# A spectral network on one NeuronCore: the product of unit 0 moved from the small products' step to the head of the products to times, with an order edge

## The chip, the cores and the metric

The kernel runs on one core of one Trainium2 chip. The metric is the device time of one execution in microseconds (us); lower is better. Three runs of the kernel before took 821.88, 822.1 and 817.92 us, a median of 821.88 us. One more execution, the one that the profiler recorded, took 814.48 us; the time from its first to its last instruction (the span) is 812.7 us. All positions below are microseconds from the start of that span.

The engines are PE (TensorE, matrix products), DVE (VectorE), ACT (ScalarE), POOL (GpSimd) and SP, which issues the DMAs. Each works through a list of its own in order and waits at an instruction until what it needs is there.

## The reference, cut to what matters

```python
def A(x, w_r, w_i):                       # x is 2048 x 512
    X = rfft2(x) * (w_r + 1j * w_i)
    return irfft2(X, s=(2048, 512))

def B(u, log_A_real, A_imag, C_real, C_imag, log_dt, D_skip):
    dt = exp(log_dt)
    A = -exp(log_A_real) + 1j * A_imag
    C = (C_real + 1j * C_imag) * dt[:, None]
    P = exp((A * dt[:, None])[:, :, None] * arange(2048))
    K = 2.0 * einsum("dn,dnl->dl", C, P).real          # one long filter for each channel
    y = irfft(rfft(u.T, 4096) * rfft(K, 4096), 4096)[:, :2048]
    return y.T + u * D_skip

x = x + A(layernorm(x))
x = x + B(layernorm(x))
x = x + A(layernorm(x))
x = x + B(layernorm(x))
```

Layer A is a filter in the two-dimensional spectrum. Layer B convolves each of the 512 channels with its own filter, as a product of spectra. All inputs are float32.

## The kernel before

Every Fourier transform is written out as products with constant matrices. The work that the change touches is in layer B, `layer_b`, which runs twice. It goes over four blocks of 128 channels each. For one block:

1. **Rows forward** (four groups, from `forward_b`): PE multiplies the normalised rows with a constant (`p<-t,w` in the first layer B, `p<-t,x` in the second), and ACT copies the result to a tile `z` (L643).
2. **Turns**: eight transposes on DVE (L649).
3. **Pairs** (four: 0 to 3; the "small products' step" is what `weigh` does for one of them): PE multiplies the turned tile with the constant `mb` (`p<-z,mb`, two results for each pair); DVE multiplies them with the spectrum of the filter (L953, four products for each pair, in tiles `wb`; one more small one, L955, in pairs 0 and 2); and four half-tile sums and differences (L964, L965) make the product spectrum `Y`. One of these four is made on DVE and three on POOL, by a table of letters, `YB`. Pairs 0 and 1 fill the first half of `Y` (j = 0), pairs 2 and 3 the second half (j = 1).
4. **The product of unit 0** (L968): one small product with the constant `MIX`, which repairs column 0 of one half of `Y`, and a copy back by ACT (L969). It comes once for each half, and stands in `weigh` after pair 0 and after pair 2.
5. **Units**, the "products to times" (`units` in `back`): eight for each block, four for each half. A unit is 16 small products `p<-mb,u` and a copy by ACT (L978). A unit of a half needs both of its pairs and the repaired column 0.
6. **Rows back** (four groups, `p<-u,t`): PE, then DVE adds the result to the residual (L992).

What sets the order: `layer_b` hands lists of steps to `interleave`, which spreads the shorter ones evenly between the longer ones, three times for a block. First come pairs 0 and 1 with the rows of the next block and the rows back of the last one; then pairs 2 and 3 with the rest of the next block's rows and the first `UH` units; then the turns of the next block with the remaining units. A scheduler turns that into one list for each engine. `issue_after(x)` is an edge that makes an instruction stand behind `x` in its engine's list; it adds no waiting by itself. In the first layer B further steps are spread through these three places (`fill`): the rest of the making of the filters (`kernel_time`, with the lines L819 to L876) and the filters' own forward transforms (`kernel_freq`). The second layer B has no such filling.

The results of PE lie in PSUM buffers: in both layers B two for rows forward, three for pairs, and three that the product of unit 0, the units and the rows back share.

Of the kernel before, what the change touches and what calls it, by code (L numbers as in the profile page):

```python
# [55 lines left out]
WB = 7  # L56
FS = [0.22, 0.37]
FH = 0.7
UH = 6
YB = 'ggvgggvg'  # L60
RNP = 'g'
KP = 0
S1 = 0
# [185 lines left out]
class Net:  # L249
# [376 lines left out]
    def forward_b(self, src, T, tag="z"):  # L626

        nc = self.nc
        tiles = {}

        def rows(n0):


            if n0 == 0:
                tiles["z"] = self.sb("z", [64, 2, 2, 8, 2])
            xs = [src(n0 + i) for i in range(4)]
            ps = [self.ps("p1", [64, 2, 2, 2]) for b in range(2)]
            self.side_by_side([(ps[b][64 * c:64 * c + 64, :, j, m], xs[2 * m + c][64 * b:64 * b + 64, 64 * j:64 * j + 64],
                                T[64 * b:64 * b + 64, n0 + 2 * m + c].rearrange("p (u r) -> p u r", r=2))
                               for m in range(2) for j in range(2) for c in range(2) for b in range(2)])  # L640
            m = n0 // 2
            for b in range(2):
                nc.scalar.copy(tiles["z"][:, :, :, b, m:m + 2].rearrange("p u j m r -> p (u j) (m r)"),  # L643
                               ps[b].rearrange("p u j m r -> p (u j) (m r)"))

        def turn(u):
            if u == 0:
                tiles["zt"] = self.sb(tag, [64, 2, 32])
            nc.vector.transpose(tiles["zt"][:, u:u + 8].rearrange("p u j d -> p (u j d)"),  # L649
                                tiles["z"][:, u:u + 8].rearrange("p u j b m r -> p (u j b m r)"))  # L650

        MB = split(self.small[:, 0:256], "slm", [2, 2, 64])

        def pair(i, use):
            last = None
            for pl in range(2):
                p = self.ps("p2", [512])
                products = []
                for h in (1, 0):
                    o = p[64 * h:64 * h + 64].rearrange("p (u d) -> p u d", d=32)  # L660
                    u = 32 * (i % 2) + 16 * h
                    c = 1 if u == 0 else 0
                    z = tiles["zt"][:, :, i // 2]
                    products += [(o[:, 0], MB[:, 0, pl], z[:, 0])] * c + [(o[:, c:], MB[:, 1, pl], z[:, u + c:u + 16])]
                last = self.side_by_side(products, last)
                use(pl, p)

        return ([partial(rows, n0) for n0 in range(0, 16, 4)], [partial(turn, u) for u in range(0, 64, 8)],
                [partial(pair, i) for i in range(4)])
# [264 lines left out]
    def layer_b(self, kf, T, out, x=None, src=None, first=None, more=(), fill=(), switch=(), kept=None, after=None):  # L934
# [3 lines left out]
        nc = self.nc  # L938
# [5 lines left out]
        def weigh(blk, Y, pairs, i):  # L944
# [14 lines left out]
            for h in range(2):  # L959
# [3 lines left out]
                e = [nc.vector if c == "v" else eng for c in YB[i % 2 * 4 + 2 * h:i % 2 * 4 + 2 * h + 2]]  # L963
                e[0].tensor_sub(y[0:64], v[0, 0], v[1, 1])  # L964
                e[1].tensor_add(y[64:128], v[0, 1], v[1, 0])  # L965
            if i % 2 == 0:
                pm = self.ps("p3", [32])
                nc.tensor.matmul(pm, MIX, Y[:, :, i // 2, 0], start=True, stop=True)  # L968
                nc.scalar.copy(Y[:, :, i // 2, 0], pm)  # L969

        def back(blk, Y):
            V = self.sb("u", [32, 2, 2, 32])

            def units(j, d):
                p = self.ps("p3", [64, 8])
                self.side_by_side([(p[64 * r:64 * r + 64, :, i], Y[:, d + i, j], MBT[:, 64 * r:64 * r + 64])
                                   for i in range(8) for r in range(2)])
                nc.scalar.copy(V[:, :, j, :, d:d + 8].rearrange("p n q d -> p q n d"),  # L978
                               p.rearrange("p (q n) d -> p q n d", q=2))
# [29 lines left out]
        last = []  # L1009
# [188 lines left out]
```

## Time and profile before

| | us |
|---|---|
| median of three runs | 821.88 |
| profiled execution | 814.48 |
| its span | 812.7 |
| first layer A, with most of the filters' making | 0 to about 280 |
| first layer B with the rest of the filters | about 280 to 556 |
| second layer A | about 556 to 691 |
| second layer B, four blocks | 691 to 812.7 |

| engine | busy, us | share of the span |
|---|---|---|
| PE | 635.4 | 78% |
| DVE | 650.3 | 80% |
| ACT | 429.6 | 53% |
| POOL | 403.3 | 50% |

Busy time is summed over the whole span. The shares are means over stages with different limits, so which engine holds a stage back has to be read in that stage. In the rows of a timeline the columns are the start, how long the group took, the engine, the line, the operation, what is written and read with its shape, and how many instructions were merged; a bracket gives the idle time of the engine before it and what ended that.

### The profile page before, as it was taken

Reading aid. Unit: us, or ns where it says so; the run is one execution under the profiler, and the core shown is the slowest. Engines: PE = TensorE matmul, PEld = TensorE weight load, DVE = VectorE, ACT = ScalarE, POOL = GpSimd, SP = SyncE. Lnnn points to the kernel's source line nnn. Section 1 sums busy time; section 2 is a strip of 40 time slices with the busy share of each in tenths; the row PEclk is TensorE's granted clock in tenths of the full one; section 3 lists DMA queues with packets and bytes.
Section 4 is the critical chain, followed back from the end, with each engine's and each line's share of the span. In section 5 each row is a group of like instructions: output and inputs, shape, how many; then the busy total and the mean of one; then the engine's idle time right before and its main releaser. Section 6 shows DMA issues by size and latency. Waiting matters only on the chain. (4 is left out here: it accounts for less than half of the span.)

```text
span 812.7 us, 18848 instructions
## 1 busy us (share of the span) xinstructions
PE 635.4 (78%) x7232; PEld 442.6 (54%) x7232; DVE 650.3 (80%) x1307; ACT 429.6 (53%) x918; POOL 403.3 (50%) x594
## 2 busy tenths in 40 slices
PE   3347788896767877997789968665899896897786
PEld 2336666664444435653356637344877663475566
DVE  7999659799998969679797868667587796976783
ACT  3424778756566955776578614213765345233212
POOL 3675876746624154613366444180056571763752
PEclk9657999999989979999699989888999997999998
DMA  8200742353556331460335456303123013322512
GB/s 313 107 0 15 159 96 79 80 139 111 130 155 142 113 54 36 106 182 19 60 86 141 147 121 186 132 21 106 53 79 81 26 40 117 105 88 75 154 44 62
DMA packets 144609, 80.49 MB, mean 99 GB/s; under 512 B 78500, under 2 KB 124200, under 8 KB 143624
## 3 DMA queue, kind: packets, MB, share of 16 engines
q1 hardware_dynamic: 144264, 78.77, 35.0%
q8 instruction: 57, 0.93, 0.5%
q0 software_dynamic: 256, 0.52, 0.4%
q14 instruction: 32, 0.26, 0.1%
HBM read 54.77 MB, written 25.03 MB: 98 GB/s over the span
## 5 line engine op out<-in xcount | busy, mean ns | idle before, releaser
L965 POOL TENSOR_TENSOR u<-wb,wb 64x512 f32<-64x512 f32 x64 | 91.3, 1427 | 118.8 <-DVE wb L953 105.8
L318 PE MATMUL p<-z,mb 128*64 128x512 f32 (+1 forms) x480 | 106.2, 558 | 16.9 <-DVE z L649 9.7
L953 DVE TENSOR_TENSOR wb<-p,kk 128x512 f32<-128x512 f32 x128 | 81.2, 680 | 18.9 <-PE p L318 17.6
L864 PE MATMUL pv<-qp 128*64 128x128 f32 x1024 | 79.9, 295 | 13.8 <-DVE qp L853 10.8
L643 ACT COPY z<-p 128x512 f32<-128x512 f32 x96 | 51.7, 594 | 69.0 <-PE p L318 60.9
L853 DVE TENSOR_TENSOR qp<-qp,mag 128x1024 f32<-128x1024 f32 x64 | 84.4, 1324 | 0.9
L864 PEld LDWEIGHTS pv<-qp 128*64 128x64 f32 x1024 | 61.3, 145 | 40.3 <-issue 9.7
L318 PEld LDWEIGHTS p<-mb,u 128*64 128x64 f32 x2048 | 71.0, 150 | 20.3 <-POOL u L964 12.6
L318 PE MATMUL p<-mb,u 128*64 128x64 f32 x2048 | 74.1, 236 | 10.1 <-POOL u L964 9.6
L851 DVE SCALAR_TENSOR_TENSOR qp<-qp,mag 128x256 f32<-128x256 f32 x128 | 65.3, 527 | 16.2 <-ACT qp L794 15.9
L528 DVE TENSOR_TENSOR w<-wt,p 128x514 f32<-128x514 f32 x64 | 42.6, 687 | 32.0 <-PE p L318 25.2
L649 DVE STREAM_TRANSPOSE z<-z 128x512 f32<-128x512 f32 x96 | 58.3, 675 | 9.7 <-ACT z L643 9.6
L978 ACT COPY u<-p 128x512 f32<-128x512 f32 x64 | 37.6, 587 | 53.6 <-PE p L318 53.6
L533 POOL TENSOR_TENSOR w<-w,w 64x257 f32<-64x257 f32 x48 | 40.0, 834 | 51.4 <-DVE w L528 45.7
L318 PEld LDWEIGHTS p<-z,mb 128*64 128x64 f32 x480 | 36.0, 146 | 51.9 <-issue 26.9
L458 PE MATMUL p<-w,w 128*128 128x128 f32 x128 | 32.0, 428 | 41.1 <-DVE w L451 38.8
L1063 POOL TENSOR_SCALAR w<-w,norms 128x128 f32<-128x128 f32 x64 | 38.1, 606 | 38.3 <-DMA w<-h 38.1
L832 DVE TENSOR_SCALAR kw<-pk 128x512 bf16<-128x512 f32 x64 | 43.3, 681 | 11.8 <-PE pk L830 11.7
L458 PEld LDWEIGHTS p<-w,w 128*128 128x128 f32 x128 | 27.7, 318 | 45.2 <-issue 24.7
L794 ACT ACTIVATE kf<-pk 128x512 f32<-128x512 f32 x64 | 38.9, 607 | 22.0 <-PE pk L833 21.6
L964 POOL TENSOR_TENSOR u<-wb,wb 64x512 f32<-64x512 f32 x32 | 46.2, 1445 | 2.3
L794 ACT ACTIVATE qp<-kf,half 128x512 f32<-128x512 f32 x64 | 47.2, 738 | 0.0
(198 smaller groups left out, 1523.4 us busy)
## 6 DMA issues: line engine op xcount, KB each, us to landing
wt<-in_w SPq DMA_DIRECT2D x32, 257.0 KB
w<-h SPq DMA_DIRECT2D x32, 256.0 KB
kf<-kk SPq DMA_DIRECT2D x32, 256.0 KB
kk<-kf SPq DMA_DIRECT2D x32, 256.0 KB
u<-in_x SPq DMA_DIRECT2D x16, 256.0 KB
hr<-in_x SPq DMA_DIRECT2D x16, 256.0 KB
kt<-stage SPq DMA_DIRECT2D x32, 128.0 KB
h<-hr SPq DMA_DIRECT2D x16, 256.0 KB
```

What stands on the lines that cost most here:

```text
L318: last = self.nc.tensor.matmul(out, weights, data, start=True, stop=True, skip_group_check=True).ins
L458: nc.tensor.matmul(p[:, b], xf[:, b], t, start=True, stop=True)
L643: nc.scalar.copy(tiles["z"][:, :, :, b, m:m + 2].rearrange("p u j m r -> p (u j) (m r)"), ps[b].rearrange("p u j m r -> p (u j) (m r)"))
L649: nc.vector.transpose(tiles["zt"][:, u:u + 8].rearrange("p u j d -> p (u j d)"), tiles["z"][:, u:u + 8].rearrange("p u j b m r -> p (u j b ...
L794: last["x"] = nc.scalar.activation(*a, **k).ins
L832: nc.vector.tensor_scalar(whole, p, MAGIC, -MAGIC, op0=ALU.add, op1=ALU.add)
L851: nc.vector.scalar_tensor_tensor(QP[:, c, 0], QP[:, c, 1, :, ::-1], -1.0 if c else 1.0, m[:, 0], op0=ALU.mult, op1=ALU.mult)
L853: nc.vector.tensor_mul(t, t, mag[:, None, 1:3, 256 * j:256 * j + 256].to_broadcast([128, 2, 2, 256]))
L864: nc.tensor.matmul(p[64 * t:64 * t + 64, g], QP[:, c, 2, d:d + 2].rearrange("p s a -> p (s a)"), QP[:, c, 0:2, d:d + 2].rearrange("p k s b ...
L953: nc.vector.tensor_mul(split(m[c, pl], "du", [32, 16]), by_channel(p), split(k[c], "du", [32, 16]))
L964: e[0].tensor_sub(y[0:64], v[0, 0], v[1, 1])
L965: e[1].tensor_add(y[64:128], v[0, 1], v[1, 0])
```

## The change

The product of unit 0 and its copy leave `weigh`. They now stand at the head of the first unit of each half (d = 0), with an edge behind the last matrix product of the pair issued most recently (`self.paired`, set in `forward_b`). `UH` goes from 6 to 4: all four units of the second half now stand with the next block's turns. `YB` still gives one of the four sums of each pair to DVE, but it is now the difference of the tile's lower half (h = 0), where it was that of the upper half.

```diff
-UH = 6
-YB = 'ggvgggvg'
+UH = 4
+YB = 'vgggvggg'
...
                 last = self.side_by_side(products, last)
                 use(pl, p)
+            self.paired = last
...
                 e[0].tensor_sub(y[0:64], v[0, 0], v[1, 1])
                 e[1].tensor_add(y[64:128], v[0, 1], v[1, 0])
-            if i % 2 == 0:
-                pm = self.ps("p3", [32])
-                nc.tensor.matmul(pm, MIX, Y[:, :, i // 2, 0], start=True, stop=True)
-                nc.scalar.copy(Y[:, :, i // 2, 0], pm)
-
         def back(blk, Y):
             V = self.sb("u", [32, 2, 2, 32])

             def units(j, d):
+                if d == 0:
+
+                    pm = self.ps("p3", [32])
+                    with self.tc.issue_after(self.paired):
+                        nc.tensor.matmul(pm, MIX, Y[:, :, j, 0], start=True, stop=True)
+                    nc.scalar.copy(Y[:, :, j, 0], pm)
```

No instruction is added or taken away; their order on the engines changes. The lists are the same up to the middle of the first block of the first layer B.

First place: PE in the third block of the second layer B. `p<-mb,u` is a unit, `p<-u,mb` the product of unit 0 (here that of the second half), the two rows `p<-z,mb` are pair 3, and `p<-t,x` are rows forward of the next block, of which only the one next to the others is shown. Before:

```order
L318 MATMUL p_1758_8333<-t_6922,x_6926 64x64x2
L318 MATMUL p_1747_8286<-mb_2602,u_8149 64x64 x16
L968 MATMUL p_1756_8329<-u_8149,mb_2602 128x32
L318 MATMUL p_1759_8352<-mb_2602,u_8149 64x64 x16
L318 MATMUL p_1764_8410<-z_8104,mb_2602 64x512 x2
L318 MATMUL p_1767_8417<-z_8104,mb_2602 64x512 x2
L318 MATMUL p_1760_8370<-mb_2602,u_8149 64x64 x16
L318 MATMUL p_1761_8388<-mb_2602,u_8149 64x64 x16
L318 MATMUL p_1770_8428<-t_6922,x_6926 64x64x2
```

Behind the last row stand the rest of that group of rows forward and then the four units of the second half. In the changed kernel pair 3 stands behind three units of the first half, with no product of unit 0 ahead of it but that of the first half:

```order
L318 MATMUL p_1757_8330<-t_6922,x_6926 64x64x2
L318 MATMUL p_1747_8286<-mb_2602,u_8149 64x64 x16
L318 MATMUL p_1758_8349<-mb_2602,u_8149 64x64 x16
L318 MATMUL p_1759_8367<-mb_2602,u_8149 64x64 x16
L318 MATMUL p_1762_8389<-z_8065,mb_2602 64x512 x2
L318 MATMUL p_1765_8396<-z_8065,mb_2602 64x512 x2
L318 MATMUL p_1768_8407<-t_6922,x_6926 64x64x2
```

The group of rows forward that begins in the last row here is followed by the fourth unit of the first half, and only then comes the product of unit 0 of the second half (L975 in the changed file):

```order
L318 MATMUL p_1769_8408<-t_6922,x_6926 64x64x2
L318 MATMUL p_1770_8427<-mb_2602,u_8149 64x64 x16
L975 MATMUL p_1772_8447<-u_8149,mb_2602 128x32
L318 MATMUL p_1773_8450<-mb_2602,u_8149 64x64 x16
L318 MATMUL p_1774_8470<-mb_2602,u_8149 64x64 x16
L318 MATMUL p_1775_8490<-mb_2602,u_8149 64x64 x16
L318 MATMUL p_1776_8510<-mb_2602,u_8149 64x64 x16
L318 MATMUL p_1781_8545<-z_8445,mb_2602 64x512
```

So the product of unit 0 of the second half moved from ahead of pair 3 to behind it, and two more units of the first half stand ahead of pair 3. Ahead of these units the block has two groups of rows forward where it had three. In the second block one more group stands between L975 and the four units; that one is the third block's first, which the third block then no longer has.

Second place: PE at the end of the fourth block, where no rows forward follow. Pair 3, the units and the products of unit 0 stood like this:

```order
L318 MATMUL p_1815_8729<-z_8484,mb_2602 64x512 x2
L318 MATMUL p_1818_8736<-z_8484,mb_2602 64x512 x2
L318 MATMUL p_1800_8625<-mb_2602,u_8529 64x64 x16
L968 MATMUL p_1809_8668<-u_8529,mb_2602 128x32
L318 MATMUL p_1810_8671<-mb_2602,u_8529 64x64 x16
L318 MATMUL p_1811_8689<-mb_2602,u_8529 64x64 x16
L318 MATMUL p_1812_8707<-mb_2602,u_8529 64x64 x16
L318 MATMUL p_1821_8747<-mb_2602,u_8529 64x64 x16
```

Three more units of the second half follow. In the changed kernel all four units of the first half stand ahead of L975:

```order
L318 MATMUL p_1813_8708<-z_8445,mb_2602 64x512 x2
L318 MATMUL p_1816_8715<-z_8445,mb_2602 64x512 x2
L318 MATMUL p_1800_8625<-mb_2602,u_8529 64x64 x16
L318 MATMUL p_1809_8668<-mb_2602,u_8529 64x64 x16
L318 MATMUL p_1810_8686<-mb_2602,u_8529 64x64 x16
L318 MATMUL p_1819_8726<-mb_2602,u_8529 64x64 x16
L975 MATMUL p_1820_8744<-u_8529,mb_2602 128x32
L318 MATMUL p_1821_8747<-mb_2602,u_8529 64x64 x16
```

Three units moved ahead of the product of unit 0; the end of the fourth block of the first layer B changes in the same way.

Third place: PE early in the first block of the first layer B. `L833` (L834 in the changed file) is a product of the filters' making, on which ACT and then DVE go on. Before, the product of unit 0 of the first half stood ahead of it:

```order
L830 LDWEIGHTS th_2963
L830 MATMUL pk_3112<-kb_599,th_2963 128x256
L968 MATMUL p_729_3076<-u_3021,mb_2602 128x32
L833 LDWEIGHTS ni_601
L833 MATMUL pk_3050<-kw_3049,ni_601 128x512
L833 LDWEIGHTS ni_601
L833 MATMUL pk_3112<-kw_3111,ni_601 128x512
```

In the changed kernel it is gone from here:

```order
L831 LDWEIGHTS th_2963
L831 MATMUL pk_3109<-kb_599,th_2963 128x256
L834 LDWEIGHTS ni_601
L834 MATMUL pk_3050<-kw_3049,ni_601 128x512
L834 LDWEIGHTS ni_601
L834 MATMUL pk_3109<-kw_3108,ni_601 128x512
```

It moved some 70 rows further back, behind pair 1 and the group of products L865 (L864 before). On POOL the order in each pair stays two sums (L965) and one difference (L964). On DVE the difference of pair 0 now stands behind two of pair 1's products instead of ahead of them.

## The prediction

> **What bounds the kernel now.** I read the busy times of the page first, then the busy times by stage, then the waits of PE, then the timeline of one block, engine by engine. Over the whole span no engine is full:
>
> ```profile
> PE 635.4 (78%) x7232; PEld 442.6 (54%) x7232; DVE 650.3 (80%) x1307; ACT 429.6 (53%) x918; POOL 403.3 (50%) x594
> ```
>
> The stages differ. The columns are the stretch, its length, the busy us (and instructions) of PE, weight loads, DVE, ACT and POOL, PE's granted clock, the DMA share and GB/s:
>
> ```profile
> 400.00:440.00 40.00, 35.42 (x552) 23.89 (x552) 35.85 (x51) 29.32 (x56) 25.70 (x25) 0.91 0.41 94
> 722.00:752.00 30.00, 25.69 (x494) 18.30 (x492) 22.38 (x35) 9.41 (x18) 16.63 (x13) 0.94 0.36 108
> ```
>
> In the first layer B, with its filling, PE and DVE are both near 90%. In the second layer B (one block in the second row) PE is busy 25.69 of 30 us, DVE 22.38 and POOL 16.63: nobody is full, so a chain of waits sets the time. The waits of PE in the second layer B (who waited for whom, us in total, times, longest):
>
> ```profile
> PE p L968 <- POOL u L964: 10.7, 5, 3.2
> PE p L318 <- POOL u L964: 6.5, 4, 2.6
> ```
>
> PE waits 17.2 us for POOL, most of it at the product of unit 0. One block shows how. It begins at 747.26 with pair 0 and the next begins at 777.63:
>
> ```profile
> 747.26 2.01 PE L318 MATMUL p<-z,mb 128*64 128x32 f32 x12
> 749.20 1.10 PE L318 MATMUL p<-t,x 64*64 64x128 f32 x32
> ...
> 760.30 1.15 PE L318 MATMUL p<-mb,u 128*64 128x64 f32 x32
> 763.58 0.42 PE L968 MATMUL p<-u,mb 128*128 128x32 f32 x2 [2.12 <-POOL u L964]
> 763.93 1.15 PE L318 MATMUL p<-mb,u 128*64 128x64 f32 x32
> 764.91 1.89 PE L318 MATMUL p<-z,mb 128*64 128x512 f32 x8
> ...
> 772.30 5.50 PE L318 MATMUL p<-mb,u 128*64 128x64 f32 x128 [2.60 <-POOL u L964]
> 777.63 2.87 PE L318 MATMUL p<-z,mb 128*64 128x32 f32 x16
> ```
>
> A unit is 32 instructions here. PE has the first unit done at 761.45, then stands at the product of unit 0 of the second half, which needs pair 2 from POOL; pair 3 (764.91), which needs nothing of that, stands behind it. POOL and DVE in the same block:
>
> ```profile
> 750.44 2.97 POOL L965 TENSOR_TENSOR u<-wb,wb 64x512 f32<-64x512 f32 x2 [7.02 <-DVE wb L953]
> 757.55 1.62 POOL L964 TENSOR_TENSOR u<-wb,wb 64x512 f32<-64x512 f32 x1
> 767.96 2.95 POOL L965 TENSOR_TENSOR u<-wb,wb 64x512 f32<-64x512 f32 x2 [4.43 <-DVE wb L953]
> 770.98 1.26 POOL L964 TENSOR_TENSOR u<-wb,wb 64x512 f32<-64x512 f32 x1
> 765.99 2.48 DVE L953 TENSOR_TENSOR wb<-p,kk 128x512 f32<-128x512 f32 x4 [3.61 <-PE p L318]
> ```
>
> POOL has pair 1 done at 757.55 + 1.62 = 759.17, then makes pair 2 and stands idle 4.43 us until DVE has products of pair 3 for it. So the loop is: POOL's pair 2, product of unit 0, a unit, pair 3 on PE, on DVE, on POOL, then the units of the second half. The block before shows the same places:
>
> ```profile
> 717.26 2.01 PE L318 MATMUL p<-z,mb 128*64 128x32 f32 x12
> 734.90 3.40 PE L318 MATMUL p<-z,mb 128*64 128x512 f32 x8
> 743.47 3.95 PE L318 MATMUL p<-mb,u 128*64 128x64 f32 x128 [2.10 <-POOL u L964]
> ```
>
> **Second and third block.** The change adds and removes no instruction; each of its edits is worth what it moves.
>
> Before, pair 3 starts 764.91 - 747.26 = 17.65 us into its block (734.90 - 717.26 = 17.64 in the other). In the changed list PE reaches pair 3 after what it did from 747.26 to 761.45 (14.19 us), less one group of rows forward (1.10), plus two more units at 3.95 / 4 = 0.99 each: 14.19 - 1.10 + 1.98 = **15.07 us**, 2.58 us sooner. The three units need pair 1 from POOL, ready at 759.17 - 747.26 = 11.91; PE comes to the first of them at 14.19 - 1.15 - 1.10 = 11.94, so they fit with nothing to spare. What follows pair 3 keeps its length: from its start to the units of the second half 772.30 - 764.91 = 7.39 us, and from these to the next block 747.26 - 743.47 = 3.79. The block becomes 15.07 + 7.39 + 3.79 = 26.25 us instead of 28.83 by the same rows. That is 2.58 us for each of two blocks, 5.2.
>
> The cover of the moved work: one group of rows forward, one unit and the product of unit 0 now run while POOL makes pair 3. They take about 1.1 + 1.0 + 0.4 of 7.39 us, beside pair 3's own 1.89, and in the second block one group more, 1.1. PE then waits once, 7.39 - 1.9 - 1.1 - 1.0 - 0.4 = 3.0 us in the third block and 1.9 in the second, where it waited twice. What is late next is POOL's pair 3, which no PE order shortens. If the cover were gone, the units would start later by what is left uncovered, at most these 3.6 us. The turns (eight on DVE) need the last rows forward, which in the second block move to just ahead of the units; their ACT copies and 4.87 us on DVE lie beside the wait and the four units:
>
> ```profile
> 770.85 4.87 DVE L649 STREAM_TRANSPOSE z<-z 128x512 f32<-128x512 f32 x8 [1.07 <-ACT z L643]
> ```
>
> Moving the DVE difference from the upper to the lower half keeps one on DVE and three POOL operations for each pair, and the sums that start first on POOL are the same; I cost it at nothing, with DVE's free 7.6 us of the 30 as cover. If it is not free, it costs a DVE difference ahead of pair 3's products, about 1.1 us a block. The edge is an order alone: nothing, and ACT's copy of unit 0 moves with the product. SP's issues of filter spectra and outputs are shuffled; the spectra are fetched a block ahead, so nothing again.
>
> Clock. Both blocks are longer than 28.83 (30.00 and 30.37), and the granted clock (the third figure from the end) says why:
>
> ```profile
> 734.00:738.00 4.00, 4.00 (x40) 1.78 (x42) 1.29 (x2) 0.80 (x2) 0.00 (x0) 0.64 0.18 47
> 772.00:778.00 6.00, 5.70 (x132) 5.59 (x134) 3.72 (x7) 1.91 (x4) 0.24 (x1) 0.72 0.01 3
> 795.00:800.00 5.00, 5.00 (x98) 5.00 (x98) 1.07 (x1) 1.29 (x3) 3.42 (x3) 0.50 0.01 3
> ```
>
> Two of the four waits were followed by a slow stretch. The first stretched 734.90 to 743.47 to 8.57 instead of 7.39 (1.18 us), the second 772.30 to 777.63 to 5.33 instead of 3.79 (1.54 us). With one wait a block I keep the second, since the third block's wait gets longer, and take back the first: 1.2.
>
> **First block and the ends.** In the first block of the second layer POOL is never idle, so its units of the second half start when POOL is done, as before: nothing. At the end of the fourth block:
>
> ```profile
> 794.23 0.64 PE L968 MATMUL p<-u,mb 128*128 128x32 f32 x2 [3.24 <-POOL u L964]
> 794.80 9.09 PE L318 MATMUL p<-mb,u 128*64 128x64 f32 x224
> 797.29 1.26 POOL L964 TENSOR_TENSOR u<-wb,wb 64x512 f32<-64x512 f32 x1
> ```
>
> POOL ends at 798.55, the units at 803.89. The changed list does the first half's four units while POOL makes pair 2, and the second half's from 798.55. At full clock these take 3.95 and end at 802.5, 1.4 us sooner; at the clock of the row 795 to 800 (98 instructions in 5 us, 1.63 us a unit) they end at 805.1, 1.2 later. The wait ahead of them grows from 3.24 to about 4 us, and 3.24 was followed by a clock of 0.50, so I take nothing, and -1.4 to +1.2 as bounds, here and at the end of the first layer B, which has the same rows.
>
> The Trainium skill bears on this ("TensorE: Matmul & The Clock Gate", Part 1): after an idle window of about 3.4 us the array falls to half clock and needs about as long of sustained work to come back. By that rule the ends would cost about 1.2 us each rather than nothing. The trace agrees with the 3.24 us row, but it also shows 0.64 behind a wait of 2.12, which is shorter than the rule's window.
>
> **First layer B, with the filling.** The first product of unit 0 stands ahead of products of the filters' making, on which ACT and then DVE wait; a later one likewise:
>
> ```profile
> 293.40 0.41 PE L968 MATMUL p<-u,mb 128*128 128x32 f32 x2 [1.24 <-POOL u L964]
> 294.13 0.60 ACT L794 ACTIVATE kf<-pk 128x512 f32<-128x512 f32 x1
> 296.67 0.42 DVE L851 SCALAR_TENSOR_TENSOR qp<-qp,mag 128x256 f32<-128x256 f32 x1 [3.40 <-ACT qp L794]
> 416.42 0.67 DVE L832 TENSOR_SCALAR kw<-pk 128x512 bf16<-128x512 f32 x1
> 417.07 0.42 PE L968 MATMUL p<-u,mb 128*128 128x32 f32 x2 [1.97 <-POOL u L964]
> ```
>
> At 293 the whole line PE, ACT, DVE shifts; of the wait of 1.24 I take 0.9, since the chain of the filters also needs DVE's own step just ahead. At 417 the product behind needs DVE's 416.42 + 0.67 = 417.09 anyway, so only unit 0's 0.42 goes: 0.4. Together 1.3. The reordering of the DVE and PE lists around it I cannot price by rows: at best both waits go whole (3.2), at worst DVE gains one wait like its 3.40.
>
> **Sum.** 5.2 + 1.2 + 0 + 0 + 1.3 = 7.7 us. The profiled execution took 814.48 us (span 812.7 and 1.8 around it), so it would take 806.8. The median of the runs is 821.88, 7.4 us above the profiled execution; I take the same difference off it: **814.2 us**, -0.9%. A measurement of this kernel can tell about 0.5% (4.1 us) from no change.
>
> **Rivals.**
> - *DVE takes the wait's place.* Pair 3's products come sooner, but DVE is still at earlier work. From pair 0's first product, about 1.1 us into the block, its list holds 12 products of 0.65, three differences of 1.1, four row sums of 0.67 and two small ones: about 1.1 + 7.8 + 3.3 + 2.7 + 0.4 = 15.3 us, and pair 3's first result is there at about 16.1. A margin of 0.8 us speaks for it, since row sums wait for PE; the 22.38 of 30 speak against. If it halves the gain of both blocks and leaves the filled part as it is: 2.6 + 0 = 2.6, about **819.3**.
> - *Half clock behind every gathered wait* (slower). It decides from a wait of about 3.2 us, as in the row 794.23. If all eight blocks then ran 5 us at 0.50, that is 8 x 2.5 = 20 us; 1.18 + 1.54 + 2 x 2.5 = 7.7 of these are there now, so 12.3 more, against 5.2 + 1.3 gained at full clock: +5.8, **827.7**. For it: the third block's 3.0 and the ends' 4. Against it: 1.9 in the second block, no idle POOL in the first, and other work on PE in the filled blocks.
>
> That the product isn't moved is no rival: the lists show it moved.
>
> **How the numbers follow.** Forecast 0.73, DVE 0.18, half clock 0.09. The forecast's own range: at best 5.2 + 2.7 (both slow stretches) + 2 x 1.4 + 3.2 = 13.9, 808.0; at worst 5.2 - 2 x 1.2 + 1.3 = 4.1, 817.8. To leave out no more than 2 in 10 I go up to 820.5, over most of the DVE case, and down to 807.5. Faster by over 0.5% (under 817.8) 0.73, within 0.5% 0.18, slower 0.09.
>
> **What would show it.** Right: in blocks two and three pair 3 starts about 15 us after pair 0, the distance between blocks is 26 to 28 us, PE's wait for POOL at the product of unit 0 is near zero, and one wait of 2 to 3 us stands ahead of the units of the second half. DVE's case: pair 3 is early on PE and DVE's products of it start without waiting for PE. Half clock: a clock near 0.5 behind each such wait. The forecast is wrong if the filled part of the first layer B, 280 to 470, moves by more than 3 us either way, or if the block's first units wait for POOL's pair 1.

## The result and the profile after

| | before | changed |
|---|---|---|
| median of six runs each, us | 816.95 | 807.67 |
| lowest and highest | 815.57 to 822.1 | 801.0 to 815.74 |
| profiled execution, us | 814.48 | 813.32 |
| its span | 812.7 | 811.5 |

The ratio of the two is **0.9848**, with a 95% interval of 0.9803 to 0.9893: 1.5% faster, about 12 us, where 7.7 us (0.9%) were forecast. The comparison leaves out the two slowest of the six runs of the changed kernel, and the profiled one is among these; so the profile of a second set of runs of the same kernel (the first experiment, 810.41 us, span 808.6) is read beside it. The medians of all six runs are 9.3 us apart (a ratio of 0.9886).

The page's row of busy times hardly shows the change:

```profile
PE 640.9 (79%) x7231; PEld 450.0 (55%) x7232; DVE 644.8 (79%) x1307; ACT 428.4 (53%) x918; POOL 406.0 (50%) x594
```

**The second layer B.** PE's part of the timeline, third block of the first profile of the changed kernel (L975 is the product of unit 0):

```profile
745.90 2.87 PE L318 MATMUL p<-z,mb 128*64 128x32 f32 x16
...
756.93 0.42 PE L975 MATMUL p<-u,mb 128*128 128x32 f32 x2
...
761.16 1.89 PE L318 MATMUL p<-z,mb 128*64 128x512 f32 x8
762.98 1.10 PE L318 MATMUL p<-t,x 64*64 64x128 f32 x32
764.01 1.15 PE L318 MATMUL p<-mb,u 128*64 128x64 f32 x32
765.09 0.42 PE L975 MATMUL p<-u,mb 128*128 128x32 f32 x2
768.55 6.65 PE L318 MATMUL p<-mb,u 128*64 128x64 f32 x128 [3.04 <-POOL u L965]
775.03 2.87 PE L318 MATMUL p<-z,mb 128*64 128x32 f32 x16
```

Pair 3 starts 761.16 - 745.90 = 15.26 us into the block (forecast 15.07, before 17.65). The product of unit 0 has no bracket any more. One wait of 3.04 us stands ahead of the four units of the second half (forecast 3.0). So the order did what was forecast. But from the start of the four units to the next block it took 775.03 - 768.55 = 6.48 us, where the forecast had 5.33. The same wait and units in the second block of this profile, and below them the granted clock there (a stretch of the windows, the clock third from the end):

```profile
740.73 5.34 PE L318 MATMUL p<-mb,u 128*64 128x64 f32 x128 [2.01 <-POOL u L965]
```

```profile
740.40:743.80 3.40, 3.07 (x58) 3.07 (x60) 2.58 (x5) 1.05 (x3) 0.27 (x1) 0.50 0.00 0
```

And in the second profile of the same kernel:

```profile
741.39 3.95 PE L318 MATMUL p<-mb,u 128*64 128x64 f32 x128 [2.02 <-POOL u L965]
```

```profile
740.40:743.80 3.40, 2.41 (x82) 2.41 (x84) 3.24 (x6) 0.66 (x2) 0.94 (x1) 1.00 0.02 5
```

The list and the wait are the same, 2.01 and 2.02 us; the clock behind it is 0.50 once and 1.00 once. In the second profile the second block takes 26.45 us, 0.2 from the forecast 26.25.

**The first layer B.** Its first three blocks by stretches, from one block's first product on DVE to the next's (the columns as in the prediction: length, busy us of PE, weight loads, DVE, ACT and POOL, then the granted clock). Before:

```profile
285.10:379.70 94.60, 78.42 (x995) 47.92 (x992) 76.19 (x129) 64.15 (x121) 37.76 (x44) 0.91 0.35 85
379.70:472.20 92.50, 79.44 (x1035) 49.80 (x1034) 79.61 (x133) 59.98 (x116) 50.34 (x57) 0.91 0.40 97
472.20:527.00 54.80, 38.49 (x627) 26.95 (x629) 38.10 (x75) 18.30 (x34) 19.60 (x17) 0.88 0.56 151
```

Changed, first and second profile:

```profile
291.90:381.40 89.50, 74.96 (x1005) 47.84 (x1001) 75.66 (x131) 63.14 (x120) 38.92 (x44) 0.93 0.37 90
381.40:471.50 90.10, 76.89 (x1029) 48.18 (x1027) 76.53 (x130) 60.16 (x115) 50.41 (x57) 0.94 0.42 101
471.50:525.10 53.60, 38.90 (x627) 26.73 (x629) 36.82 (x74) 18.21 (x34) 19.67 (x17) 0.87 0.55 152
```

```profile
289.70:382.30 92.60, 76.96 (x1014) 48.65 (x1012) 76.11 (x131) 63.67 (x120) 38.77 (x44) 0.92 0.36 87
382.30:474.20 91.90, 79.69 (x1030) 49.66 (x1027) 76.94 (x131) 60.03 (x115) 50.46 (x57) 0.91 0.41 99
```

The first two blocks together went from 187.1 us to 179.6 and to 184.5. The prediction had put its limit for this part at 3 us: in one of the two profiles it moved by 7.5. Also, everything ahead of 285 us has the same lists in both kernels, and still the first product came 6.8 and 4.6 us later here. A single profile is no measure for this kernel; the table below therefore joins profiles of kernels that have the same list in a stage. Distances in us, worked out from the starts of the blocks' first product on DVE and the last addition of rows back:

| stage | list of before | changed list | difference of the means |
|---|---|---|---|
| first layer B, first two blocks | 187.1, 189.9, 187.7, 188.2 | 179.6, 184.4, 180.5, 184.5, 179.7 | -6.5 |
| its last two blocks | 87.8, 88.5, 88.6 | 87.0, 87.7, 87.6, 87.6 | -0.9 |
| second layer B, first block | 24.7, 24.4, 24.6 | 26.0, 24.7, 26.2, 26.0 | +1.1 |
| second and third block | 60.4, 63.6, 60.4 | 57.0, 54.4, 56.0, 55.6 | -5.7 |
| fourth block | 30.3, 28.9, 30.3 | 31.7, 30.8, 30.8, 30.8 | +1.2 |

The profiles are those of before and of the changed kernel, and of e1, e5, e6, e7, e8, e13 and e15 below wherever the stage's list is one of the two. The sum is -10.8 us, 1.3%. Each mean stands on three to five profiles, and the 63.6 of e6 alone makes 1.1 us of the -5.7.

### The profile page after: what moved, and what is told of

It is laid out like the page before. It is cut to its first block, busy times and chain, and to the rows that moved or that the text cites. A ratio compares the mean times of both kernels' runs of the same rounds, so it can differ in the third digit from the quotient of the medians.

```text
span 811.5 us, 18861 instructions
## 1 busy us (share of the span) xinstructions
PE 640.9 (79%) x7231; PEld 450.0 (55%) x7232; DVE 644.8 (79%) x1307; ACT 428.4 (53%) x918; POOL 406.0 (50%) x594
## 5 line engine op out<-in xcount | busy, mean ns | idle before, releaser
L966 POOL TENSOR_TENSOR u<-wb,wb 64x512 f32<-64x512 f32 x64 | 93.1, 1454 | 106.9 <-DVE wb L954 99.7
L318 PE MATMUL p<-mb,u 128*64 128x64 f32 x2048 | 78.5, 246 | 20.0 <-POOL u L965 19.5
L318 PEld LDWEIGHTS p<-mb,u 128*64 128x64 f32 x2048 | 75.2, 160 | 28.9 <-POOL u L965 23.3
L865 PE MATMUL pv<-qp 128*64 128x128 f32 x1024 | 77.8, 292 | 10.3 <-DVE qp L854 8.8
L865 PEld LDWEIGHTS pv<-qp 128*64 128x64 f32 x1024 | 61.1, 145 | 38.1 <-issue 16.8
L854 DVE TENSOR_TENSOR qp<-qp,mag 128x1024 f32<-128x1024 f32 x64 | 80.4, 1260 | 0.9
L852 DVE SCALAR_TENSOR_TENSOR qp<-qp,mag 128x256 f32<-128x256 f32 x128 | 64.6, 522 | 16.6 <-ACT qp L795 16.5
L318 PEld LDWEIGHTS p<-z,mb 128*64 128x64 f32 x480 | 37.6, 147 | 55.1 <-issue 25.1
L649 DVE STREAM_TRANSPOSE z<-z 128x512 f32<-128x512 f32 x96 | 58.3, 671 | 9.0 <-ACT z L643 9.0
L795 ACT ACTIVATE kf<-pk 128x512 f32<-128x512 f32 x64 | 38.9, 607 | 33.0 <-PE pk L834 30.9
L458 PEld LDWEIGHTS p<-w,w 128*128 128x128 f32 x128 | 28.5, 327 | 44.8 <-issue 23.9
L833 DVE TENSOR_SCALAR kw<-pk 128x512 bf16<-128x512 f32 x64 | 43.1, 680 | 8.2 <-PE pk L831 8.1
L546 PE MATMUL p<-ca,w 128*128 128x128 f32 x256 | 41.5, 294 | 7.3 <-DVE w L535 2.5
```

The lines of the kernel that those rows point to most:

```text
L318: last = self.nc.tensor.matmul(out, weights, data, start=True, stop=True, skip_group_check=True).ins
L458: nc.tensor.matmul(p[:, b], xf[:, b], t, start=True, stop=True)
L795: last["x"] = nc.scalar.activation(*a, **k).ins
L833: nc.vector.tensor_scalar(whole, p, MAGIC, -MAGIC, op0=ALU.add, op1=ALU.add)
L852: nc.vector.scalar_tensor_tensor(QP[:, c, 0], QP[:, c, 1, :, ::-1], -1.0 if c else 1.0, m[:, 0], op0=ALU.mult, op1=ALU.mult)
L854: nc.vector.tensor_mul(t, t, mag[:, None, 1:3, 256 * j:256 * j + 256].to_broadcast([128, 2, 2, 256]))
```

## The experiments

The ratio is always to the kernel before, run on the same chip in the same set, with its 95% interval.

**The changed kernel again (e1).** No edit.

> The changed kernel as it is, for a second look at where its time goes. Theory (gain from the removed waits at the product of unit 0): the distances between first products of the blocks of the second layer B come out near those of the first profile, 26.0, 27.9 and 29.1 us (24.7, 30.0 and 30.4 before), and those of the first layer B stay below the kernel before's by 5, 2 and 1 us (94.6, 92.5 and 54.8 before). Rival (what the first layer B gained is chance of that one execution): its distances come back to within 1 us of those of before. What happens ahead of the first product (285.1 before, 291.9 after) should differ by chance only, in either direction.

Measured: 811.4 against 820.49 us, ratio 0.9897 (0.9855 to 0.994). Together with the first comparison the gain is 1.0 to 1.5%. The second profile shown above is from here. By its first layer B the rival would be nearer than the theory: the three distances are 2.0, 0.6 and 0.5 us below those of before, where 5, 2 and 1 were expected. The times of the runs keep the gain all the same.

**Which layer it comes from (e5, e6, e7).** `layer_b` knows which of its two calls it is in. e5 makes all edits in the second layer B alone, e6 all in the first alone, e7 only the move with its edge, in the second alone. The lines are those of e5; in e6 the first of them has `not second`, and e7 has `second, False, 6`:

```diff
+        second = src is None
+        NEW_MIX, NEW_YB, uh = second, second, 4 if second else 6
...
+            if i % 2 == 0 and not NEW_MIX:
+                pm = self.ps("p3", [32])
+                nc.tensor.matmul(pm, MIX, Y[:, :, i // 2, 0], start=True, stop=True)
+                nc.scalar.copy(Y[:, :, i // 2, 0], pm)
...
-                if d == 0:
+                if d == 0 and NEW_MIX:
```

> All three edits in the second layer B alone; the first layer B has the lists of the kernel before. Theory (the removed waits of PE shorten the second and third block): distances between the blocks' first products 24.7, 26.5 and 27.9 us and 30.8 to the end, against 24.7, 30.0, 30.4 and 30.3 before; the total falls by 5 to 6 us, ratio 0.993, less where half-clock stretches fall on the waits. Rival (the gain comes from the first layer B): ratio 0.998 to 1.002.

> All three edits in the first layer B alone; the second layer B has the lists of before. Theory (what remains of the measured gain of 8 to 12 us comes from here, because the making of the last filter ends sooner): from the first product to the last copy of the filters 175 to 180 us against 184 before, and the total 3 to 6 us below before, ratio 0.993 to 0.996. Rival (it was chance): 184 us, ratio 0.998 to 1.002.

> Only the move of the product of unit 0 with its edge, and only in the second layer B; UH 6 and the old YB there, the first layer B as before. Theory: this move carries the gain of the second layer B, and a fourth unit ahead of pair 3 costs back 1.0 us in each of two blocks: 27.4 and 27.9 to 28.9 us for the second and third block, total 3 to 4 us below before, ratio 0.995 to 0.997, so that its loss as a whole-kernel edit came from the first layer B. Rival (the move alone doesn't help the second layer B): second block 28.8 us or more, as in the profile of that edit alone, ratio 1.0.

Measured: e5 0.9962 (0.9933 to 0.9991), e6 **0.9877** (0.9843 to 0.991), e7 0.9965 (0.9937 to 0.9994). Of 820 us that is 3.1 us from the second layer, 10.1 from the first, and 2.9 from the move alone in the second. The forecast had it the other way round: 6.4 of 7.7 in the second layer, 1.3 in the first. e6 gained more than its theory had (3 to 6 us). e5 came out between theory and rival. The ratio of e7 is the theory's, but its profile is the rival's: 29.1 and 30.1 us for the second and third block, and 115.5 us for all four (115.3 before). So the gain of the move alone in the second layer rests on a ratio whose interval ends just under 1.

**Which edit it takes (e2, e3, e9, e10), in both layers.**

```diff
 e2: the move alone        e3: UH alone       e9: move and YB      e10: move and UH
 UH = 6                    UH = 4             UH = 6               UH = 4
 YB = 'ggvgggvg'           YB = 'ggvgggvg'    YB = 'vgggvggg'      YB = 'ggvgggvg'
```

> Only the move of the product of unit 0 with its edge; UH is 6 again and YB is the old table. Here four units instead of three stand ahead of pair 3. Theory: the move makes nearly all of the gain, less about 1 us for the fourth unit in each of two blocks, so 9 to 12 us below the kernel before, ratio 0.985 to 0.990. Rival (UH or YB makes the gain): ratio above 0.995.

> Only UH 4; the product of unit 0 stays in weigh, the old YB. Theory: pair 3 still stands behind the product of unit 0 of the second half, so PE's waits there stay and the blocks of the second layer B keep 28.5 to 30.5 us; ratio 0.997 to 1.002. Rival (moving two units beside the turns is what counts): second and third block under 28 us, ratio under 0.993.

Measured: e2 **1.0061** (1.0032 to 1.0089), e3 **1.0114** (1.0073 to 1.0155). Each of the two parts alone makes the kernel slower. e2 missed its theory (0.985 to 0.990), and e3 lies outside theory and rival alike. Both profiles lose in the first layer B: 285.1 and 288.1 us from its first product to its end, where the kernel before has 274.8 and the changed one 266.6 and 272.1. e2 loses in its last two blocks (96.0 us, before 87.8), e3 in the first two (194.5, before 187.1) and in the last two (93.6). DVE's list in e2, at the change from the second to the third block, shows a difference that the prediction did not speak of:

```profile
464.20 4.86 DVE L649 STREAM_TRANSPOSE z<-z 128x512 f32<-128x512 f32 x8 [0.24 <-ACT z L643]
468.99 1.39 DVE L852 SCALAR_TENSOR_TENSOR qp<-qp,mag 128x256 f32<-128x256 f32 x4
470.29 2.35 DVE L854 TENSOR_TENSOR qp<-qp,mag 128x1024 f32<-128x1024 f32 x2
477.92 1.89 DVE L954 TENSOR_TENSOR wb<-p,kk 128x512 f32<-128x512 f32 x3 [5.27 <-PE p L318]
488.26 0.28 DVE L909 TENSOR_TENSOR w<-w,dsk 1x128 f32<-1x128 f32 x1 [8.46 <-DMA w<-kt]
```

In the kernel before, the same place reads:

```profile
465.47 1.36 DVE L853 TENSOR_TENSOR qp<-qp,mag 128x1024 f32<-128x1024 f32 x1
467.38 4.86 DVE L649 STREAM_TRANSPOSE z<-z 128x512 f32<-128x512 f32 x8 [0.56 <-ACT z L643]
472.17 1.85 DVE L953 TENSOR_TENSOR wb<-p,kk 128x512 f32<-128x512 f32 x3
480.49 0.28 DVE L908 TENSOR_TENSOR w<-w,dsk 1x128 f32<-1x128 f32 x1 [6.48 <-DMA w<-kt]
```

And in the changed kernel:

```profile
464.03 1.22 DVE L854 TENSOR_TENSOR qp<-qp,mag 128x1024 f32<-128x1024 f32 x1
466.76 4.86 DVE L649 STREAM_TRANSPOSE z<-z 128x512 f32<-128x512 f32 x8 [1.50 <-ACT z L643]
471.55 1.84 DVE L954 TENSOR_TENSOR wb<-p,kk 128x512 f32<-128x512 f32 x3
478.50 0.28 DVE L909 TENSOR_TENSOR w<-w,dsk 1x128 f32<-1x128 f32 x1 [5.11 <-DMA w<-kt]
```

L852 and L854 (L851 and L853 before) are the last steps of the filters' making. Behind them come PE's sums, an ACT copy, the filter's way through memory (`kt`) and back, and the addition of `d_skip` (L909, L908 before), ahead of which DVE stands still. In e2, e3 and e9 the eight turns of the third block (L649) stand ahead of the last filter steps and delay that chain; in the kernel before, in the changed kernel and in e10 they stand behind. From that came the theory for e9 and e10.

> The move with its edge and the new YB, with UH back at 6, in both layers. In DVE's list of the first layer B the eight turns of the third block stand ahead of the last two filter steps here, as they do with the move alone; in the changed kernel and in the kernel before they stand behind them. Theory (the place of these turns decides the first layer B, and YB does nothing): like the move alone, ratio 1.000 to 1.010, first layer B (first pair product to last addition) 281 us or more, the last filter's staging copy over 185 us behind the first pair product. Rival (YB brings the gain of the first layer B): ratio 0.985 to 0.995, first layer B under 276.

> The move with its edge and UH 4, with YB as before, in both layers. In DVE's list the turns stand behind the last filter step, as in the changed kernel. Theory (list, not YB): like the changed kernel, ratio 0.983 to 0.993, first layer B 266 to 276 us. Rival (YB brings the gain): ratio 0.998 or more, first layer B over 277.

Measured: e9 1.0051 (1.0021 to 1.008), first layer B 281.6 us; e10 0.9917 (0.9884 to 0.995), first layer B 271.0. Both as the theory had it. The gain takes the move and `UH` together: the first two blocks take 183.5 us in e10, 189.1 in e2 and 194.5 in e3. `YB` isn't needed for it; whether it adds the last 0.2 to 0.7% between e10 and the changed kernel, these intervals can't tell.

**The place of the turns by itself (e11, e12).** e2 and e3 with an edge that puts these turns (the transpose of L649) behind the last filter step:

```diff
-            nc.vector.tensor_mul(t, t, mag[:, None, 1:3, 256 * j:256 * j + 256].to_broadcast([128, 2, 2, 256]))
+            x = nc.vector.tensor_mul(t, t, mag[:, None, 1:3, 256 * j:256 * j + 256].to_broadcast([128, 2, 2, 256]))
+            self.term = x.ins if (i, j) == (units[-1], 1) else None
...
+            with ExitStack() as stack:
+                if getattr(self, "term", None) is not None:
+                    stack.enter_context(self.tc.issue_after(self.term))
```

> The move with its edge alone (UH 6, YB as before), as in the run of that name, and one more edge: the turns of the third block of the first layer B stand behind the last filter step in DVE's list; nothing else is different. Theory (the place of the turns cost the move alone its gain): first layer B falls from 285 to 277 us or less, the staging copy comes at most 184 us behind the first pair product, ratio 0.985 to 0.998. Rival (the move itself, or the wait for POOL at another place, costs it): ratio stays at 1.003 to 1.009, first layer B over 282.

> UH 4 alone with the same additional edge. Theory: first layer B falls from 288 to 281 us or less, ratio from 1.011 to between 0.997 and 1.005. Rival (four units that stand late in each block cost it, whatever the turns do): ratio stays at 1.007 to 1.015, first layer B over 285.

Measured: e11 1.0033 (1.0006 to 1.0059), e12 1.001 (0.9982 to 1.0038). With `UH` alone the loss is gone (from 1.0114, the intervals are apart), though its profile's first layer B fell only from 288.1 to 285.0 us, where 281 was expected; the last two blocks fell from 93.6 to 89.6 us, the first two did not (195.4), and the profiled execution was the slowest of its twelve. With the move alone the profile's first layer B fell as expected, from 285.1 to 275.7, but the ratio only from 1.0061 to 1.0033, with intervals that overlap: the expected 0.998 was missed. So the turns' place is a part of it. What was left in e11, again on DVE:

```profile
469.32 4.85 DVE L652 STREAM_TRANSPOSE z<-z 128x512 f32<-128x512 f32 x8
474.10 1.25 DVE L958 TENSOR_TENSOR wb<-p,kk 128x512 f32<-128x512 f32 x2
475.79 0.69 DVE L958 TENSOR_TENSOR wb<-p,kk 128x512 f32<-128x512 f32 x1 [0.44 <-PE p L318]
483.86 0.28 DVE L913 TENSOR_TENSOR w<-w,dsk 1x128 f32<-1x128 f32 x1 [7.38 <-DMA w<-kt]
```

Behind three products of the third block DVE waits 7.38 us for the last filter's rows, and the other thirteen products, which need nothing of it, wait behind.

**The addition out of the way (e13, e14, e15).** An edge puts the `d_skip` addition of the fourth filter behind the third block's products, in the changed kernel, in e11 and in the kernel before:

```diff
-                    nc.vector.tensor_mul(split(m[c, pl], "du", [32, 16]), by_channel(p), split(k[c], "du", [32, 16]))
+                    x = nc.vector.tensor_mul(split(m[c, pl], "du", [32, 16]), by_channel(p), split(k[c], "du", [32, 16]))
+                    self.product = x.ins
...
+                    with ExitStack() as stack:
+                        if blk in (3,) and getattr(self, "product", None) is not None:
+                            stack.enter_context(self.tc.issue_after(self.product))
```

(e14 and e15 name the third filter too, where the order stays as it was.)

> The changed kernel with one more edge: the addition of d_skip to the last filter (L909 there), at which DVE stood 5.1 us for the DMA of the filter's rows, stands behind the sixteen products of the third block's pairs instead of behind three of them. Theory (the first layer B is gated by the last filter's making, and DVE's list passes that wait on to the pairs): the wait of DVE there goes to under 1 us, the distance from the third block's first product to the fourth's falls from 54 to 47-51 us, ratio 0.975 to 0.985. Rival (the fourth block needs that filter anyway, so the wait only changes its place): that distance stays at 53 to 57 us, ratio 0.984 to 0.993.

> The move with its edge alone, the turns behind the last filter step, and the d_skip addition late as well. Theory: the 7.4 us that DVE stood at this addition go from the pairs: third to fourth block 48 to 53 us instead of 56.5, ratio 0.987 to 0.999. Rival: the distance stays at 55 us or more, ratio 1.000 to 1.006.

> The kernel before with the late d_skip addition alone. Theory: DVE stood 6.5 us there, the third block's distance falls from 54.8 to 48-51 us, ratio 0.990 to 0.996. Rival (the fourth block needs the filter anyway): 54 us or more, ratio 0.997 to 1.004.

Measured: e13 **0.9806** (0.9758 to 0.9854), 804.23 us; e14 0.991 (0.9871 to 0.9949); e15 0.9975 (0.9944 to 1.0007). The distance from the third to the fourth block is 50.3, 51.6 and 50.8 us, within the theory's numbers each time. DVE's timeline in e13, and the stretch of the third block:

```profile
470.09 1.85 DVE L957 TENSOR_TENSOR wb<-p,kk 128x512 f32<-128x512 f32 x3
471.98 0.21 DVE L960 TENSOR_TENSOR wb<-p,kf 64x32 f32<-64x32 f32 x1
...
483.65 0.33 DVE L912 TENSOR_TENSOR w<-w,dsk 1x128 f32<-1x128 f32 x1
```

```profile
470.10:520.40 50.30, 37.80 (x627) 27.68 (x629) 35.80 (x74) 18.21 (x34) 20.17 (x17) 0.90 0.60 164
```

The wait is gone, and the addition comes 13.6 us behind the third block's first product instead of 7.0, without harm: what the fourth block needs has that much room. So this layer was held at that point by DVE's list, not by the filter itself. e13 is the fastest of all kernels run; its interval overlaps that of the first comparison and ends just under that of e1 (0.9854 and 0.9855), and its profile saves 3.3 us at the place where it should (50.3 instead of 53.6). The time of e15 is the rival's (0.997 to 1.004), and its interval includes 1, though its profile's stage did what the theory expected. So for the kernel before, the saving in the stage isn't shown in the time.

**The clock (e4, e8).** The product of unit 0 of the second half is repeated into the same place, so that PE has work while it waits: six times in both layers (e4), or 10, 10, 15 and 21 times in the four blocks of the second layer B alone (e8). The lines are those of e4:

```diff
-                    with self.tc.issue_after(self.paired):
-                        nc.tensor.matmul(pm, MIX, Y[:, :, j, 0], start=True, stop=True)
+                    for _ in range(6 if j else 1):
+                        with self.tc.issue_after(self.paired):
+                            self.paired = nc.tensor.matmul(pm, MIX, Y[:, :, j, 0], start=True, stop=True, skip_group_check=True).ins
```

> The changed kernel, with the product of unit 0 of each second half issued six times into the same result instead of once, 2.1 us of work for PE inside the wait that stands ahead of the second half's units. Theory (half clock behind the gathered wait eats gain in the second layer B): these four units take about 4.0 us instead of the 5.3 to 6.7 of the first profile, the blocks of the second layer B come down to 24.5, 26.3 and 26.6 us, and the total falls by 5 to 8 us below the changed kernel's. Rival (the clock follows something else): the units keep 5 to 6.5 us and the total stays within 2 us, or rises by the added work.

> The changed kernel, with the product of unit 0 of the second half issued 10, 10, 15 and 21 times in the four blocks of the second layer B, so that PE works through nearly all of the gathered waits of 2.0, 2.3, 3.0 and 4.4 us. The first layer B keeps the changed kernel's lists. Theory (a gathered wait brings half clock, and half clock lengthens the units behind it): the four units behind each wait take 4.0 us in all four blocks, 24.7, 26.5, 26.5 and 29.2 us for the four distances, 3 us below the best profile of the changed kernel. Rival (half clock comes regardless, from the weight loads and small products in the window): the units behind the waits of the third and fourth block keep 5.4 us, and the total equals the changed kernel's within 1 us.

Measured: e4 0.9941 (0.9912 to 0.997), e8 0.9842 (0.9805 to 0.988). In e4 the second layer B has the same blocks as in e1 (26.45, 27.95 and 30.77 us), so six of these small products didn't help: waits of 1.92 and 3.30 us were left in the third and fourth block, and half clock followed both. Its first layer B got other lists throughout and took 275.8 us, 272.1 in e1. In e8 PE hardly stands still ahead of the second half's units (0.27 us in the first block, 0.39 in the fourth); the rows are the units of the third and the fourth:

```profile
770.03 3.97 PE L318 MATMUL p<-mb,u 128*64 128x64 f32 x127
...
793.64 5.50 PE L318 MATMUL p<-mb,u 128*64 128x64 f32 x128 [0.39 <-issue]
```

The third block's units ran at full clock (5.44 us in e1). But the scheduler also put the whole pair 0 of the fourth block ahead of them, so it isn't the filled wait alone that differs. The second and third block took 51.4 us together, where e1 had 54.4, and the fourth 33.8 instead of 30.8: the layer as a whole is no shorter than in e1 (110.3 and 109.8). That the waits cost clock fits e8, and isn't shown by it; filling them in this way brings nothing in all.

## Why the prediction was right and wrong

- **Second and third block, 5.2, and clock, 1.2:** the order was right. Pair 3 came at 15.26 and 15.28 us, and at full clock the second block is as forecast (26.45). The clock's part held in one profile of four: the slow stretch of the second block was to go, and it went in e1, but not in the first profile, e5 and e13 (units of 5.34, 5.50 and 5.42 us instead of 3.95). The means of the table give 5.7 of 6.4.
- **First block and the ends, 0:** wrong by 2.3 us in the second layer. The first block's units also stand behind one gathered wait now, which the prediction did not see, since it looked only at when POOL is done. Before, that time was in two waits, of 2.17 and 1.02 us; now it is one of 2.23 to 2.26. It was followed by half clock in three of four profiles, and not in any of three before. The fourth block lost 1.2 us, the bound that the prediction had worked out for it and set against a gain of 1.4 that didn't come.
- **First layer B, with the filling, 1.3:** this is the step that failed: a term put at 1.3 us that measured 7.4 by the table and 10.1 by e6 (7.4 to 12.9). It priced two waits and said: "The reordering of the DVE and PE lists around it I cannot price by rows: at best both waits go whole (3.2)". That "at best" was no bound, because it held only the waits that the change removes by its own hand, while the scheduler wrote new lists for the whole filled part. The wait at 293 us went about as priced (3.40 to 2.47 us). In the first two blocks PE had three waits at the product of unit 0 (1.24 and 1.97 us, and one of 0.99 at 316.7 that the prediction left out); all three are gone in both profiles of the changed kernel. Even so PE's idle time there, the length less the busy time, only went from 29.2 to about 27.8 us in both. Some of the rest shows in DVE's groups in the first two blocks, before and in the first profile of the changed kernel (busy us, mean ns of one, then the idle time ahead):

```profile
L853 DVE TENSOR_TENSOR qp<-qp,mag 128x1024 f32<-128x1024 f32 x33 | 45.3, 1381 | 0.6
L832 DVE TENSOR_SCALAR kw<-pk 128x512 bf16<-128x512 f32 x32 | 21.7, 682 | 10.3 <-PE pk L830 10.3
L926 DVE TENSOR_SCALAR kf<-kk,kc 64x32 f32<-64x32 f32 x4 | 0.9, 234 | 4.5 <-ACT kk L918 4.5
```

```profile
L854 DVE TENSOR_TENSOR qp<-qp,mag 128x1024 f32<-128x1024 f32 x33 | 41.3, 1256 | 0.6
L833 DVE TENSOR_SCALAR kw<-pk 128x512 bf16<-128x512 f32 x32 | 21.6, 682 | 6.7 <-PE pk L831 6.6
L927 DVE TENSOR_SCALAR kf<-kk,kc 64x32 f32<-64x32 f32 x4 | 1.3, 315 | 1.9 <-ACT kk L919 1.9
```

  The same 33 filter steps cost 4.1 us less on an engine that is busy for 83% of this part, and two groups of waits 6.2 us less (10.3 to 6.7 and 4.5 to 1.9). The waits differ between profiles: in the second one it is 4.3 us less, and DVE's idle time as a whole is 31.4 us there, 27.4 in the first profile and 31.3 before. The 4 us are no chance: the sum over these steps, added up from the trace's records, is 41.4 or 41.5 us in all five profiles with the changed list, and 45.6 to 46.2 in all four with the old one. But they don't decide: in e2, e3, e9 and e11, all slower than the kernel before, these steps take 41.5 to 42.3 us too.

  A rival for a part of it is the clock. With the same changed list, the first two blocks took 179.6 and 179.7 us where the clock's record has 23.9 us at 0.50, 180.5 with 27.3, and 184.4 and 184.5 with 30.9; with the old list it has 34.1, 37.6, 27.3 and 34.2 us, in the table's order. At 27.3 us the old list took 187.7 (e7) and the changed one 180.5 (e6). So the list gains without the clock too, as far as one pair of profiles shows; whether the clock sets the length or follows it stays open.

  That the new lists of the first layer gain is shown (e6). Which of their many moves gains how much stays open. The turns and the addition aren't it: they stand alike in the kernel before and in the changed one. They are a part of why the single edits lose, and the addition is where e13 found more.
- **The sum, 7.7:** 10.8 by the table. That it is no further off is in part luck: the first layer's term was 6.1 us too small, and those of the second layer 3.0 too large. The forecast time, 814.2, also stood on the three runs known then (821.88); the six runs of the kernel before have a median of 816.95. Of the 6.5 us from 814.2 to 807.67, 4.9 are this base and 1.6 the gain. From its own base the range's low end, 807.5, left room for 14.4 us.
- **The rival "DVE takes the wait's place":** did not happen. POOL now waits 1.19 and 0.97 us for DVE ahead of pairs 2 and 3, where the prediction had a margin of 0.8; the blocks kept their forecast length. **"Half clock behind every gathered wait":** it was so in all four waits of the second layer B in the first profile of the changed kernel, and from shorter waits than the 3.2 us at which the rival has it begin (2.01). But its price was far from 12.3 us: the clock's record has 20.5 us at 0.50 there and 13.7 before, which is 3.4 us of lost work at most; and two of the four kept full clock in the second profile.

## What to carry to other kernels

Where a scheduler writes the lists, the price of an edit in a stage that is nearly full is not that of the instructions it names: compare the whole list of the busiest engine at the change from block to block, above all what stands ahead of the chain that the next stage waits for. Look for an instruction that waits long for a DMA on an engine with an ordered list, and ask what behind it needs nothing of it: here one edge there brought the fastest kernel. And two parts that each lose may gain together; the single edits here (0.6 and 1.1% slower) would both have been thrown away. Where the clock comes and goes, one profile of a stage is not enough: the same list took 179.6 to 184.5 us for the same two blocks.

## What the runs showed of the hardware

**Half clock comes on a grid.** In the first profile of the changed kernel the stretches at 0.50 in the second layer B begin at 713.1, 740.4, 767.7 and 795.0 us (from the clock's own record), 27.3 us apart, and last 3.4 or 6.8 us. 27.3 is eight times 3.41. In the kernel before they begin at 735.1, 772.7 and 793.2, which is eleven and six times 3.41 apart. In the first profile the units behind the four waits start 27.7 to 28.0 us apart, so each wait falls into nearly the same place of the grid; in the second they start 26.4 to 26.5 us apart, and two of the four waits were followed by half clock. That the place on the grid decides is a reading of these rows; no run tested it. Waits of 2.0 and 2.3 us were followed by half clock in one profile and not in the other, those of 3.0 and 4.4 in both (the four units behind them took 6.65 and 6.46 us in the first, 5.44 and 5.50 in the second). The length of the wait alone doesn't decide: the one of 3.24 us in the fourth block of the kernel before was followed by half clock there, and in e6, with the same list, it wasn't. The Trainium skill ("TensorE: Matmul & The Clock Gate", Part 1) speaks of an activity window of about 3.4 us that runs freely. The grid agrees with that; that an idle time of 2.0 us can be enough is what the runs add.

**A DVE step beside POOL takes longer, or makes POOL's longer.** From the kernel before, two of the filter steps of DVE (L853) and the POOL operations beside them:

```profile
310.20 1.22 DVE L853 TENSOR_TENSOR qp<-qp,mag 128x1024 f32<-128x1024 f32 x1
...
321.22 1.91 DVE L853 TENSOR_TENSOR qp<-qp,mag 128x1024 f32<-128x1024 f32 x1
```

```profile
310.37 2.18 POOL L965 TENSOR_TENSOR u<-wb,wb 64x512 f32<-64x512 f32 x1 [4.67 <-DVE wb L953]
313.96 1.28 POOL L965 TENSOR_TENSOR u<-wb,wb 64x512 f32<-64x512 f32 x1 [1.41 <-DVE wb L955]
...
320.78 3.48 POOL L965 TENSOR_TENSOR u<-wb,wb 64x512 f32<-64x512 f32 x2 [4.13 <-DVE wb L953]
```

At 310.20 DVE was first: it took 1.22 us, as without POOL, and POOL's operation 2.18 instead of 1.28. At 321.22 POOL was first, and DVE took 1.91. That fits the Trainium skill ("SBUF — State Buffer", "Who interferes with whom"): a DVE instruction with two inputs from SBUF and a GpSimd one that reads there exclude each other, and the order of issue decides who waits. It is the likely reason for the 4.1 us above: of the 33 steps, 20 met a POOL operation before (1.48 us on average) and 16 in the first profile of the changed kernel (1.30), and the others took 1.22 in both. It wasn't tried by itself.
